# Another order table for attention in thirds and two MLPs: most GpSimd operations go to VectorE and ScalarE

## The chip, the cores and the metric

The kernel runs on one core of a Trainium2 chip. The core has TensorE (PE in the profile, and PEld for its weight loads), VectorE (DVE), ScalarE (ACT), GpSimd (POOL) and SyncE (SP), which here issues every DMA. Each engine has its own queue and takes its instructions strictly in the order in which they stand there. The metric is the device time of one execution in microseconds, the median of several runs.

## The reference, cut to what matters

```python
scores = where(mask[h], (q @ k.T) / sqrt(64), -1e9)      # 4 batches, 8 heads, 576 positions, head size 64
attn   = softmax(scores);  x = attn @ v                  # heads 0-3: 32 last positions; heads 4-7: every 4th of the last 128
x = x.transpose(0, 2, 1, 3).reshape(2304, 512)
x = square(relu(x @ w_in1)) @ w_out1                     # 512 -> 2048 -> 512
h = x @ w_in2
out = (h * sigmoid(h)) @ w_out2                          # 512 -> 2048 -> 512
```

The inputs q, k and v are float32; the weights arrive as float64, which the kernel reads as pairs of 32-bit words.

## The kernel before, in words

**Precision.** Every large matrix product runs as three matmuls of rounded 32-bit operands (fp32r): each factor is split into a high part (a copy that rounds, L238, L240 or L242, by the engine that does it) and a low part (the difference, `sub`, L245), and hi·hi, hi·lo and lo·hi are summed in PSUM. The helper lines L238 to L245 therefore hold most of the elementwise work of the kernel. The tile names tell the uses apart: `w`, `wp` and `st` are weights, `x` and `xs` activations that enter a layer, `g` the hidden activations, and `hl` and `gq` the halves and the hidden blocks in the last part.

**Weights.** A chunk of 128 x 512 float64 weights is turned into float32 in six steps (L275 to L311: scale the upper word, scale the lower word, shift, put the sign in, add the words as integers) and then split. Half of the chunks are also summed in pairs (L363, L382, L410) for products of Strassen's kind, and what is needed later goes out to DRAM (`w1s`, `w1x`, `w2s`, `w2x`, `w2y`) and is read back.

**Stages.** Stage I, from the start to 278 us: most of the attention (48 blocks, each a third of a batch and a pair of heads: scores L515, masked minimum L525, exponential L530, division L534 to L548, transpose L557, product with v L570) woven into the first MLP on its first three column tiles of 192, 320 and 256 (L645 to L695). Stage II, from 278 to 567 us: the other three tiles of the first MLP, 512 columns each, with seven products in place of eight in its first half (L793; the sums of the seven are L807 to L816 on ACT and DVE) and plain products in its second (L847 to L849). Stage III, from 567 us to the end: the second MLP in three tiles of 768 columns, with seven products of 384 columns in both halves (L951 and L1036); L922 and L927 take sums out of PSUM, L987 is the Silu, and L245 on `gq` and `hl` makes the differences and the low parts.

**What sets the order.** Nothing is decided while the kernel runs. The program first makes a list of 3840 operations without order. A text table, `ORDER`, then names them one after another: a letter for the engine (P TensorE, V VectorE, A ScalarE, G GpSimd, D a DMA on SP, F a run of warm-up matmuls), the operation's number, and behind each @ the place of a buffer in SBUF or the PSUM bank. `Planner.order` reads the table, and the operations are issued in that sequence; semaphores between engines follow from the data. Every GpSimd operation gets one wait more: for the last operation on VectorE ahead of it in the table that is marked `lock`, which are those that read or write only SBUF (`o.turn = turn` in `order`, made a dependency at the end of `run`).

Of the kernel before, what the change touches and what calls it, by code (L numbers as in the profile page):

```python
# [1216 lines left out]
G0 V1 D40@145 F15@2 P42@1@65@0 V47 D21@179 P23@0@18@1 D2@160 D59@113 D78@104 D87@196 G88@118 V43 G89 A44 V49 A50  # L1217
A48 V45 V24 A46 V51 V52 A79@154 G81 P61@1@33@3 V64 A65 V68 V28 A69 V53 V62 P4@2@149@2 V7 V26 V66 V5 A63 V9 A29
A8 V90 D350@172 D95@97 F5@3 P351@0@190@0 F14@2 G97 G96@159 G98 D146@22 G147@141 G149 V91 V92 V354 V356 P54@2
F3@1 A67 A6 A27 V70 V71 V352 V72 A25 V30 V31 A10 A80 V11 V12 D129@145 G130@91 V82 G83 G148 G84@0 V33 A355 A353  # L1220
A55 F1@1 V99 A14 V13 P15@3 V100 V16 G101@82 A32 A357 A17 V358 V359 V132 A131 V133 G134 A360 P34@0 A36 A35
D366@137 P367@3@50@2 V372 A373 V368 A369 G85 G135@86 G102 D418@36 P419@2@194@3 V422 V420 D494@114 F2@1
P495@1@128@1 F3@0 V370 A421 A423 P73@0 D163@109 A371 A164@98 D22@41 D121@179 G136 G122@144 G123 V150 V498 V496
V500 V424 V374 V151 V375 V166 V167 V165 F7@3 P361@2 F3@3 A362 A74 D3@52 P37@2 P18@3 V19@4 V20 A501 A376 A499
V168 V38 V39 A152@74 V153 A425 A497 D41@198 P56@1 A57@20 D60@133 P75@3 A76 D112@29 A114 G113@155 V426 V77 V58
D104@151 A105@65 G107 A106 P1118@2 P1124@0 A1119@107 A1120 V124 V427 V428 D138@102 G139@157 G141 G140 V502 V503
A1125@92 A505 V115 V116 V117 G118@44 G119 A1126 A1121@130 G1122 V125 V108 G109 P377@2 P363@1 A364@7 V365 V142
A378 P429@0 A169@30 A430 A1127@15 G170 G126 D382@146 P383@3@12@2 V384 D436@59 P437@2@79@3 V440 A441 V442 V438
A443 A504 V388 A389 A439 V386 V1431@90 D512@167 P513@1@68@0 V516 V390 P1130@0 A1131@165 V514 V518 A519 A1132
V444 V445 V446 P431@2 A432 V434@38 V435 P379@1 V380 V381 V433 G93@34 G94 A517 D400@53 P401@3@150@1 V402 A515  # L1230
V110@48 P447@0 V143 V111 A387 P506@1 A508 A448 A391 P1136@2 A507 A1137@191 A1138 G1139@66 D180@23 D454@109
# [12 lines left out]
A241@203 V552 V490 V491 P1148@2 A1149@196 V493 A195@52 A553 A557 G243 G226 A1150 G1151@181 V1180 G1181@169 V590
V591 A592 D214@121 V215@179 V1444@184 V233 V1440 V235 D206@23 D265@66 A267 G236 G1152 G208 G1445 P1160@3 P1172@1
V216 P593@0 A594 V244 V558 V559 P1184@2 A1185@197 A1161@14 D581 V245 P1153 V266@194 V196 V1170 P1171 A1173@80
A1186 V217 A1174 G268 G1175@145 V560 P561@1 A562 V1446@199 V1162 V218 G207@177 V209 V210 G211 G1447 V1176
A1163@181 V227 V1182 G1448 G237@125 P595@3 D248@172 A249@78 A225 G228 A212@149 D598@117 P599@2@191@3 D634@157
D1438 V219 G220@153 G1466@122 V251 V1164 V596@142 D650@129 D616@70 D1441 V1449 D1450 D188 V606 V602 V604 P563@0
V250 V564 V252 G253 G254@26 G255 A603 A605 A1451 G1452 V221 P1196@1 P1208@3 A1197@12 A1209@173 V565 V213 V269  # L1250
G270 V600 A1187@161 A601 D1453 D274@187 D86 P1165 P1177 P1190@0 P1183 V238 A607 V608 V1198 V609 V610 V1188
A229@137 A1199@15 A1191@179 A1192 G1193@183 V1210 V1467@18 G1200 G230 A1211@96 G1194 G1212 P611@1 V612 P1202@2
A1203@181 V1204 P617@0@23@0 V620 V624 A625 V622 A623 P635@3@165@1 V638 A639 V618 V640 V636 A619 A637 A621 P613@2
A614@192 P1220@1 V626 A641 A1221@90 V1222 V642 V643 P1189 P1214@2@3@0 V1454@12 A644 P645@1 A646 A1215@68
A1205@42 A1216 A1217@198 P1201 V276 V275@175 V277 V278 V627 V271@78 G272 P651@1@177@1 V652 V654 A653 V656 P647@2
V648@179 P1213 G628 P629@2 V246@96 G247 G279 P1226@1 A1227@173 A1228 A655 P1195 V630 P631@1 A632@167 D615 D120
D597 D103 D257@161 D137 D702@117 D308@145 D649 P1232@2 A1233@0 A1234 V1455@165 V1456@200 V1218 G1206 G1470@141
G1457 P1207 P1238@1 V1468@68 V1469 V258@195 G1229@64 G1458@184 V260 V1471 V259 V261 G262 A1235@171 V1236 G1459
A1460 A1475 G1476 G263@161 G1461 A1472 G1473 D282@14 V283@24 V1230 V285 V309@2 G311 A1239@72 A657 V658 V310 D633
A1240 A284 V286 G287 V659 V660 P1244@2 A1245@18 P1231 D666@121 D299@190 A1246 A1247@181 P667@1@82@1 V668 A669  # L1260
V672 V674 V300@188 V670 A671 P1250@2 A1251@179 V1252 G1253@42 P661@1 P1219 V312 A662 A673 A675 V676 V677
P703@2@13@2 V708 V706 P663@1 D291@165 D171 D222 D1477 A1223@169 A678 G264 G1463 G313 V302 A709 G1224 V664@129
P1237 D684@157 D1474 V1254 V704 A705 A707 D1462 D316@171 D665 P1262@1 A1263@196 V710 V288@44 G289 V711 V1464
P679@2 A680 V1264 V314@141 V315 P1255 P685@1@70@3 V692 A712 V690 A691 G301 P681@2 A682@147 V688 V303 G280@64
G1248 V1479@68 A693 V686 V713 V304 P1225 P1256@2 A1257@121 V1258 A293 G305@190 A1241@24 G1242 A687 A1259@178
A689 P1268@1 P1249 P714@2 V292@203 V281 P1243 V294 A1269@199 A1270 G1490@42 A716 A715 P717@2 V295 V296 V694
V1491@168 V317@145 V319 D205 D154 D720@129 G306 A1271@117 G1272 V718@182 V695 V696 P1280@1 A1281@0 A1282 P1286@2
# [257 lines left out]
```

## Time and profile before

| | |
|---|---|
| runs | 955.8, 950.17, 955.35 us (median 955.35) |
| profiled execution | 957.83 us, its span 956.0 us, mean granted TensorE clock 0.966 |
| busy PE / DVE / ACT / POOL | 884.0 / 660.0 / 393.7 / 594.4 us |
| DMA | 227.92 MB, 238 GB/s in the mean |

"Busy" is the time in which an engine has an instruction under way. Matmuls overlap one another, so that a PE that is busy all the time may still run below its best rate; the distance from one matmul's start to the next one's tells the rate. An instruction on DVE or ACT starts some 0.07 us before the recorded end of the one in front of it, so that the steady distance of a group is a little less than its duration. A group's mean holds undisturbed instructions and slowed ones alike; the smallest duration of a group is what an undisturbed one takes.

### The profile page before, as it was taken

The page shows a single profiled execution, that of the slowest core. Times are in us where ns is not written, and L with a number is a line of the kernel's source. Part 1 is how long each engine was busy: PE and PEld are TensorE (multiplying, and loading weights), DVE is VectorE, ACT ScalarE, POOL GpSimd, SP SyncE. Part 2 cuts the span into 40 slices and gives each one's busy share as a digit, 9 for nine tenths or more (in the row PEclk, how much of TensorE's full clock was granted, in tenths as well). Part 3 has the DMA queues.
Part 4 walks back from the last instruction along what each step waited for, and adds up shares of the span by engine and source line. Part 5 has one row for each costly group of instructions (what it writes and reads, how often), then busy time and mean ns, then how long its engine had stood idle before and what let it go on. Part 6 is the DMA issues. An engine that isn't in the chain of part 4 may idle for free. (4 is left out here: it accounts for less than half of the span.)

```text
span 956.0 us, 17592 instructions
## 1 busy us (share of the span) xinstructions
PE 884.0 (92%) x6317; PEld 822.5 (86%) x6317; DVE 660.0 (69%) x1288; ACT 393.7 (41%) x1071; POOL 594.4 (62%) x589
## 2 busy tenths in 40 slices
PE   7898797999899999999999978999999989999988
PEld 5698686999888887898898858898989988999978
DVE  6989968857766578776689997658862376324771
ACT  5655344555344233212211222665324654337730
POOL 5777767668755767364637788767870378503662
PEclk9778998999999999999999998999999999999999
DMA  8625567537979988877988966885676264865441
GB/s 316 229 92 189 167 210 242 174 137 246 333 241 342 321 292 290 297 261 252 337 301 301 312 240 239 322 280 206 238 287 226 96 237 160 308 234 185 154 177 67
DMA packets 87064, 227.92 MB, mean 238 GB/s; under 512 B 8640, under 2 KB 20160, under 8 KB 86976
## 3 DMA queue, kind: packets, MB, share of 16 engines
q1 hardware_dynamic: 86976, 226.79, 68.3%
q8 instruction: 50, 0.82, 0.3%
q14 instruction: 38, 0.31, 0.1%
HBM read 176.42 MB, written 50.33 MB: 237 GB/s over the span
## 5 line engine op out<-in xcount | busy, mean ns | idle before, releaser
L245 POOL TENSOR_TENSOR hl<-gq,hl 128x384 fp32r<-128x384 f32 x78 | 89.5, 1163 | 97.9 <-ACT hl L238 72.8
L951 PE MATMUL y<-xs,ws 128*128 128x384 f32 x552 | 107.4, 335 | 1.6 <-DVE gq L922 0.7
L238 ACT CAST hl<-gq 128x384 fp32r<-128x384 f32 x168 | 77.6, 512 | 72.0 <-POOL gq L245 33.5
L245 DVE TENSOR_TENSOR hl<-gq,hl 128x384 fp32r<-128x384 f32 x90 | 81.2, 931 | 27.6 <-ACT hl L238 27.5
L951 PEld LDWEIGHTS y<-xs,ws 128*128 128x128 f32 x552 | 96.4, 188 | 3.3 <-DVE gq L922 1.5
L530 ACT ACTIVATE ap<-ap,ast 128x80 f32<-128x80 f32 (+3 forms) x168 | 59.1, 353 | 66.1 <-DVE ast L525 56.3
L809 DVE TENSOR_TENSOR h<-s,h 128x512 f32<-128x512 f32 x96 | 59.4, 619 | 37.2 <-PE s L793 22.3
L848 PE MATMUL y<-g,w 128*128 128x512 f32 x192 | 77.2, 402 | 6.0 <-DVE g L245 4.6
L1036 PE MATMUL sa<-hl,wp 128*128 128x384 f32 x432 | 79.7, 336 | 2.4 <-ACT hl L238 1.1
L1036 PEld LDWEIGHTS sa<-hl,wp 128*128 128x128 f32 x432 | 75.1, 188 | 3.6 <-ACT hl L238 1.4
L245 POOL TENSOR_TENSOR gq<-gq 128x384 f32<-128x384 f32 x49 | 56.0, 1155 | 34.3 <-DVE hl L245 22.6
L245 POOL TENSOR_TENSOR g<-r,g 128x512 fp32r<-128x512 f32 (+3 forms) x54 | 62.6, 1165 | 23.4 <-ACT g L238 6.0
L793 PE MATMUL s<-x,ws 128*128 128x256 f32 x576 | 76.8, 284 | 0.3 <-DVE x L245 0.3
L847 PE MATMUL y<-g,w 128*128 128x512 f32 x192 | 76.9, 400 | 0.0
L849 PE MATMUL y<-g,w 128*128 128x512 f32 x192 | 76.3, 398 | 0.0
L922 DVE TENSOR_TENSOR gq<-y,gq 128x384 f32<-128x384 f32 x46 | 25.2, 552 | 73.8 <-PE y L951 57.3
L927 ACT COPY gq<-y 128x384 f32<-128x384 f32 x92 | 42.9, 481 | 78.5 <-PE y L951 78.2
L793 PEld LDWEIGHTS s<-x,ws 128*128 128x128 f32 x576 | 73.1, 192 | 1.7 <-DVE x L245 0.5
L645 PE MATMUL s<-x,w 128*128 128x192 f32 (+2 forms) x192 | 59.9, 312 | 4.2 <-DVE xo L240 4.2
L1036 PE MATMUL sa<-hl,sw 128*128 128x384 f32 x288 | 53.6, 339 | 9.3 <-DVE hl L245 6.5
L1036 PEld LDWEIGHTS sa<-hl,sw 128*128 128x128 f32 x288 | 49.7, 188 | 12.4 <-DVE hl L245 8.4
L242 POOL TENSOR_SCALAR g<-r 128x512 fp32r<-128x512 f32 (+3 forms) x41 | 27.3, 666 | 52.1 <-DMA raw<-w 9.2
(165 smaller groups left out, 2431.4 us busy)
## 6 DMA issues: line engine op xcount, KB each, us to landing
raw<-w SPq DMA_DIRECT2D x64, 512.0 KB, 5.8
ws<-w1x SPq DMA_DIRECT2D x48, 512.0 KB, 6.3
ws<-w2x SPq DMA_DIRECT2D x48, 512.0 KB, 6.0
sw<-w2y SPq DMA_DIRECT2D x48, 512.0 KB, 4.8
wa<-w1s SPq DMA_DIRECT2D x24, 512.0 KB, 5.7
wa<-w2s SPq DMA_DIRECT2D x24, 512.0 KB, 5.9
blk<-qkv SPq DMA_DIRECT2D x16, 512.0 KB, 6.4
w1x<-st SPq DMA_DIRECT2D x16, 512.0 KB, 5.0
```

What stands on the lines that cost most here:

```text
L238: self.nc.scalar.copy(out=out, in_=in_)
L245: self.eng[eng].tensor_tensor(out=out, in0=a, in1=b, op=ALU.subtract)
L530: es.append(self.op({"ACT": c_act(nk) + 0.185}, lambda e, i=i, c=c: nc.scalar.activation(out=p.tile[:, c], in_=p.tile[:, c], func=AF.Exp, ...
L645: nc.tensor.matmul(o, wh.tile[:, s], xh, start=(kk == 0), stop=False)
L793: nc.tensor.matmul(bank.tile[:, o:o + 256], wp, xp, start=i == 0, stop=last, skip_group_check=True)
L809: add = lambda o, a, b: nc.vector.tensor_tensor(out=o, in0=a, in1=b, op=ALU.add)
L847: nc.tensor.matmul(o, wh.tile[:, s], gh.tile, start=c == 0, stop=False)
L848: nc.tensor.matmul(o, wh.tile[:, s], gl.tile, start=False, stop=False)
L849: nc.tensor.matmul(o, wl.tile[:, s], gh.tile, start=False, stop=(c == NF - 1))
L927: return self.op({"ACT": c_actp(half)}, lambda e: nc.scalar.copy(out=out(), in_=bank.tile[:, :half]), deps, key, allocs, uses + [bank])
L951: nc.tensor.matmul(o, w[part == 2].tile[:, kk * P:kk * P + P], x[b][part == 1].tile[:, kk * half:kk * half + half], start=new and not kk a ...
L1036: nc.tensor.matmul(o, u.tile[:, c * P:c * P + P], v.tile, start=new and not q and not part, stop=q == nf - 1 and part == 2, skip_group_che ...
```

## The change

Only the table is another. The list of operations, what each computes, and all other code are the same. The new table names the same 3840 operations and the same nine runs of warm-up matmuls (53 in all).

| | operations before | after |
|---|---|---|
| TensorE, DMA | 746, 540 | 746, 540 |
| VectorE | 1120 | 1457 |
| ScalarE | 874 | 1020 |
| GpSimd | 560 | 77 |
| stage I: VectorE, ScalarE, GpSimd | 455, 331, 197 | 565, 427, 19 |
| stage II | 388, 182, 181 | 463, 222, 28 |
| stage III | 277, 361, 182 | 429, 371, 30 |

In all, 695 operations have another engine than before; 32 of them go to GpSimd. Of what leaves GpSimd, differences and sums (two operands) go to VectorE: `hl` 78 to 18 on GpSimd, `gq` 49 to 3, `w`, `wp` and `st` low parts 61 to 13, the integer adds of L311 30 to 2, the sums of L363, L382 and L410 59 to 9, the low parts of `g` 54 to 6. Rounding copies and scalings (one operand) go for the most part to ScalarE: `g` 41 to 4 on GpSimd, `st` and `w` copies 51 to 3, the two scalings of the weights 45 to 3. Of the shifts of L295/L297, 20 go from GpSimd to VectorE. In stage I the operations of VectorE grow by 110: by 60 of two operands and 512 columns, by 41 that are of one operand and 512 columns or of two operands and 256, by 22 low parts of `g`, less 13 that are for the most part copies out of PSUM given to ScalarE. No operation of TensorE is issued more than 25 places earlier or later among the 746 than before; most keep their place or move by one or two. The places of the buffers in SBUF are others throughout.

```diff
@@ ORDER @@
-G0 V1 D40@145 F15@2 P42@1@65@0 V47 D21@179 P23@0@18@1 D2@160 D59@113 D78@104 D87@196 G88@118 V43 G89 A44 V49 A50
+G0 D21@181 P23@2@8@1 V1 V24 A25 V28 V26 A29 A27 D40@137 P42@0@11@0 V43 V45 A46 A44 V47 A48 D95@166 V97 V49 A50
...
```

The first place is the conversion of the first weights, for which the first matmuls of the first MLP (L645) wait. A stretch near the start of GpSimd's queue before (`cv` a converted chunk, `raw` a chunk as loaded, `w_309` a chunk's high and low part):

```order
L285 TENSOR_SCALAR raw<-raw 128x512
L242 TENSOR_SCALAR w_309<-cv 128x512
L242 TENSOR_SCALAR w_328<-cv 128x512
L311 TENSOR_TENSOR cv<-cv,raw 128x512
L245 TENSOR_TENSOR w_309<-cv,w_309 128x512
L242 TENSOR_SCALAR w_368<-cv 128x512
L245 TENSOR_TENSOR w_328<-cv,w_328 128x512
L245 TENSOR_TENSOR w_368<-cv,w_368 128x512
```

VectorE's queue after, at the same work (`x` is the input of the first MLP, `ax` a PSUM bank of the attention):

```order
L295 TENSOR_SCALAR cv<-cv 128x512
L534 TENSOR_SCALAR ast<-ast 128x3
L245 TENSOR_TENSOR x<-ax,x 128x192
L311 ISA cv<-raw,cv 128x1024
L536 RECIPROCAL ast<-ast 128x3
L285 TENSOR_SCALAR raw<-raw 128x512
L240 CAST w_547<-cv 128x512
L245 TENSOR_TENSOR x<-ax,x 128x4x48
```

The scalings, integer adds, copies and differences of the weights now stand between the attention's steps in one queue, where before GpSimd had a good part of them in a queue of its own.

The second place is the second half of the last tile of the second MLP, where the matmuls of L1036 wait for `hl`. The end of GpSimd's queue before:

```order
L245 TENSOR_TENSOR gq<-gq 128x384 x2
L245 TENSOR_TENSOR hl<-gq,hl 128x384 x2
L245 TENSOR_TENSOR gq<-gq 128x384 x2
L245 TENSOR_TENSOR hl<-gq,hl 128x384 x5
L245 TENSOR_TENSOR gq<-gq 128x384
L245 TENSOR_TENSOR hl<-gq,hl 128x384 x6
L245 TENSOR_TENSOR gq<-gq 128x384
L245 TENSOR_TENSOR hl<-gq,hl 128x384 x3
```

VectorE's queue after, near its end (`yq` is a block of the output, summed out of PSUM):

```order
L245 TENSOR_TENSOR gq<-gq 128x384 x5
L245 TENSOR_TENSOR hl<-gq,hl 128x384 x2
L245 TENSOR_TENSOR gq<-gq 128x384
L245 TENSOR_TENSOR hl<-gq,hl 128x384 x5
L245 TENSOR_TENSOR gq<-gq 128x384
L245 TENSOR_TENSOR hl<-gq,hl 128x384 x5
L922 TENSOR_TENSOR yq<-sa,yq 128x384
L245 TENSOR_TENSOR gq<-gq 128x384
L245 TENSOR_TENSOR hl<-gq,hl 128x384 x2
```

What GpSimd and VectorE did side by side here is now nearly all in VectorE's queue, in one row with the sums out of PSUM; GpSimd keeps 7 `hl` and one `gq` of this tile.

## Rows read from the trace of the kernel before

**Rows 1.** The page, part 1: busy us, share of the span, instructions.
```profile
PE 884.0 (92%) x6317; PEld 822.5 (86%) x6317; DVE 660.0 (69%) x1288; ACT 393.7 (41%) x1071; POOL 594.4 (62%) x589
```

**Rows 2.** Busy time by stretch, I, II, III: length, engines, clock, DMA share, GB/s.
```profile
0.00:278.00 278.00, 243.93 (x2294) 223.67 (x2295) 219.70 (x584) 136.14 (x477) 195.01 (x219) 0.91 0.62 214
278.00:567.00 289.00, 279.21 (x2009) 246.42 (x2008) 221.70 (x422) 78.21 (x230) 178.30 (x180) 0.99 0.86 297
567.00:956.00 389.00, 360.89 (x2017) 352.38 (x2015) 218.57 (x284) 179.31 (x364) 221.05 (x191) 0.99 0.61 213
```

**Rows 3.** The chain of waits: start, us, work.
```profile
721.81 6.24 PE y L951 x36
```

**Rows 4.** PE in order of time: start, us, instructions.
```profile
318.14 0.40 PE L847 MATMUL y<-g,w 128*128 128x512 f32 x1
...
319.98 0.39 PE L849 MATMUL y<-g,w 128*128 128x512 f32 x1
...
410.83 3.17 PE L793 MATMUL s<-x,ws 128*128 128x256 f32 x24
413.83 0.88 PE L793 MATMUL s<-x,wc 128*128 128x256 f32 x6
```

**Rows 5.** Line L245: duration ns smallest/median/largest, first and last start, forms.
```profile
L245 DVE TENSOR_TENSOR hl<-gq,hl x90: 540/768/2176, 607.6 to 944.7; 128x384 fp32r<-128x384 f32 x90
L245 POOL TENSOR_TENSOR hl<-gq,hl x78: 996/1062/1663, 620.4 to 938.3; 128x384 fp32r<-128x384 f32 x78
L245 DVE TENSOR_TENSOR st<-st x22: 660/692/1782, 92.4 to 633.5; 128x512 fp32r<-128x512 f32 x22
```

**Rows 6.** Line L922, the same view: sums that read PSUM.
```profile
L922 DVE TENSOR_TENSOR gq<-y,gq x46: 542/556/558, 594.1 to 891.7; 128x384 f32<-128x384 f32 x46
```

**Rows 7.** DVE and POOL in order of time, second half of a tile.
```profile
788.10 6.50 DVE L245 TENSOR_TENSOR hl<-gq,hl 128x384 fp32r<-128x384 f32 x5
...
791.57 3.91 POOL L245 TENSOR_TENSOR hl<-gq,hl 128x384 fp32r<-128x384 f32 x3
...
895.13 1.03 DVE L245 TENSOR_TENSOR hl<-gq,hl 128x384 fp32r<-128x384 f32 x2 [2.44 <-ACT hl L238]
```

**Rows 8.** DVE groups of stage I: busy us, mean ns | idle before, releaser.
```profile
L307 DVE SCALAR_TENSOR_TENSOR cv<-cv,raw 128x512 int32<-128x512 int32 x16 | 19.6, 1224 | 0.6 <-POOL raw L297 0.6
L304 DVE SCALAR_TENSOR_TENSOR cv<-raw,cv 128x512 int32<-128x512 int32 x20 | 17.7, 885 | 0.3
L542 DVE TENSOR_TENSOR ap<-ap,ast 128x192 f32<-128x192 f32 (+2 forms) x21 | 16.5, 788 | 0.4
L534 DVE TENSOR_SCALAR ast<-ast 128x3 f32<-128x3 f32 (+1 forms) x34 | 15.5, 455 | 4.2 <-ACT ap L530 4.1
...
L245 DVE TENSOR_TENSOR w<-cv,w 128x512 fp32r<-128x512 f32 x14 | 14.0, 1002 | 1.5 <-POOL w L242 0.7 <-ACT w L238 0.7
L295 DVE TENSOR_SCALAR cv<-cv 128x512 int32<-128x512 int32 x20 | 12.6, 631 | 2.2 <-POOL cv L277 2.0
```

**Rows 9.** Lines L295 and L534: duration ns smallest/median/largest.
```profile
L295 DVE TENSOR_SCALAR cv<-cv x34: 412/427/1501, 10.8 to 603.2; 128x512 int32<-128x512 int32 x34
L534 DVE TENSOR_SCALAR ast<-ast x48: 134/170/1303, 7.3 to 417.3; 128x4 f32<-128x4 f32 x24, 128x3 f32<-128x3 f32 x24
```

**Rows 10.** Busy time by stretch, around the end of stage II.
```profile
504.00:576.00 72.00, 61.59 (x343) 53.85 (x342) 68.76 (x78) 15.32 (x28) 57.68 (x50) 0.96 0.80 275
```

**Rows 11.** The page, part 5: ACT's rounding copy in stage III.
```profile
L238 ACT CAST hl<-gq 128x384 fp32r<-128x384 f32 x168 | 77.6, 512 | 72.0 <-POOL gq L245 33.5 <-DVE gq L245 14.0 <-POOL hl L245 8.1
```

**Rows 12.** Whom DVE and PE waited for: us in total, times, longest.
```profile
DVE gq L922 <- PE y L951: 57.3, 20, 6.1
...
DVE hl L245 <- ACT hl L238: 27.5, 13, 4.0
DVE ap L525 <- PE ax L515: 25.6, 16, 4.6
...
PE sa L1036 <- DVE hl L245: 7.1, 7, 1.6
```

More of the change, by code (lines that the diff above doesn't have):

```diff
@@ L1222 @@
[L1222 to L1231, printed above, removed]
@@ new lines @@
+P449@2 V452 V109 A409 V520 V521 V523 A1139@12 A407 V522 V410 V411 V412 V453 A457 A186@113 P509@3 A510 V511
+P395@1 F3@0 A396 A450 A463 V1134 V1140 G187 P1142@0 A1143@170 V451 A110@48 A1144 A127@100 A459 P1154@1 A1155@92
+A1145@23 A461 A174 A1156 A173@149 A1157@163 G1158 D530@125 V111 P531@3@54@1 V536 V128 V538 A539 D197@154
+V198@146 D566@159 P567@0@151@2 V572 V570 V464 V160 V200 V532 P397@2 P1129 P1135 V175 V568 V534 V176 A144@60
+D474@199 P475@1@96@0 A199 V465 V145 V1146 P524@0 V525 A161@92 V162 A526 A537 A535 A573 V177 A569 V466 P413@3
@@ new lines @@
+P1196@3 A1197@80 P1208@1 P1153 V606 V221 V209 V241@191 A607 V243 P1165 P1171 V1176 P1177 A1187@177 A1209@200
+V1182 V210 V238 A592 P593@2 A1210 A267 A225 V211 A212@149 V251 A266@163 A1198 V244 V1444@196 V245 V213 P1183
+V1445 A605 V608 V1188 V1446@16 V609 V1447 V250 A246@96 V252 D616@70 D634@157 P635@3@180@2 V640 P617@1@193@0
+D274@64 D1441 V636 V638 V268 V622 V253 V228 A1448 A1199@174 A594 P595@0 A596@161 P1190@2 V247 V620 V610
+A1191@131 A1192 V254@26 P1202@0 A1203@186 A1204 A1205@42 P1189 V1449 A1211@171 V255 A1193@165 V618 V1194 V1200
@@ new lines @@
+P1297 D342@198 D1498 D1535@86 D324 D1501 D1554@74 A1329@176 A343@72 A1330 A1537 A1325@0 A1536@183 V1512 V1308
+P1334@1 A1335@185 P1309 V345 V339@113 D790@30 D1510 D755 V786 D1513 V767 V768 P769@2 V1531 A1331@121 A1336
+V1514@166 V1332 V1326 P1333 V346 V770 V340 V1515@23 V1516@56 P787@1 A788@14 V1517 A1337@122 P791@2@70@0 V1538
+V792 P771@1 V772@187 A793 V796 V1338 D773 P1327 V794 A795 A344 V1518@117 V1519 V1532@129 V1533 V347 V348@145
+V1539 V1540 A1523 V1524 A797 V798 D1534 D341 D806@198 D1525 D1563@179 P1310@1 A1520 A1311@5 A1312 P1340@2
@@ new lines @@
+A1341@194 A1342 A1313@68 A1343@202 P1352@1 A1353@185 A1354 V799 V800 P1346@2 A1347@86 A1348 A1349@171 V1314
+P1358@1 V1544@129 A1359@165 V349 V1556 V1541@1 V1542 A1360 P801@2 A802 P1339 P803@1 A1555@173 A804@32 V1344
+V1546@125 V1521 V1557 P807@2@88@3 V808 A809 V1350 V812 V1545 A1548 V814 A813 V810 A1355@118 V1356 P1364@1
+A1365@10 V1366 V1547 A1367@7 V1368 A815 D824@185 D805 D1958@22 P1345 P1370@2 P1376@1 A811 V816 V817 V1549 V818
+G1551 V1552 A1564@72 V1565 A1361@183 V1566 A1371@42 A1372 A1373@12 A1377@79 A1378 P819@2 A820 P1315 P1357
@@ new lines @@
+D2585 D2635@44 P2763 V1949 D2641@183 P2766 D1739 D1928 A2764 V1950@125 V2830 A2802@191 V1951 V2751 V2767 V1939
+A1952 V1953 D2642@153 P2768 D2644@195 P2770 P2772 V2773 V2817 V2824 A2765 A1955 A2805@70 V2854 V2803 V1956
+A2769@47 A2812@44 V2813 V2862 V2850 A2771@14 P2775@3 P2777 A2758 A2825@118 A2778 A2774 V2806 V2836 D2639@106
+D1905 P2779 A2780 A2781 A2851@67 A2855@80 A2808@54 A2960@41 D2645@148 P2782 D2643@77 D1954 P2784 V2785 P2804
+A2837@148 A2884@115 P2787 A2788 A2948@61 V2856 V2776 A2789 V2809 V2826 V2840 A2841@196 V2783 V2832 V2858
@@ L1461 @@
+V3762 P3768@1@3 P3771 P3774 V3822 A3823@151 V3824 A3803@16 V3804 V3764 V3728 D3729 P3777 P3780 P3783 P3786
+A3811@35 V3812 P3789 P3797 P3801 P3805 P3809 P3813 V3792 V3726 D3727 D3763 D3765 V3790 D3791 D3793 V3816 P3817
+P3821 P3825 P3828 P3829 A3826@181 D3827 P3830 P3831 P3832 P3833 P3834 P3835 A3836 D3837
 """
```

448 lines of the change are left out of this document (215 added, 233 removed).

## The prediction

> **What bounds the kernel now.** The page's first part says TensorE: it is busy for 92% of the span [rows 1]. That share hides how well it runs, so the next view is busy time by stretch for the three stages [rows 2], set against what the matmuls need at their best rate. In stage III, 36 matmuls of 384 columns follow one another in 6.24 us, 0.1733 us each [rows 3]; the stage has 2016 of them (L951 and L1036, 3 tiles x 8 pairs of chunks x 42 each; 2017 matmuls in all [rows 2]), which is 349.4 us, and it takes 389. In stage II, eight distances between matmuls of 512 columns are 319.98 - 318.14 = 1.84 us, 0.23 each, and 24 of 256 columns take 413.83 - 410.83 = 3.00, 0.125 each [rows 4]: 576 (3 tiles x 16 chunks x 12) and 1008 (3 x 8 x 42) of them are 132 + 126 = 258 us, and with the 425 small matmuls of attention left in the stage (2009 - 1584 [rows 2]), at an estimated 0.03 us, about 270; it takes 289. In stage I the 1152 large matmuls (3 tiles x 16 chunks x 24, 256 columns in the mean) are 144 us, and the rest is small ones; the granted clock is 0.91 there, against 0.99 later. With 0.91 as a mean of full and half speed, 0.18 of 278 us, 50 us, went at 1.2 GHz, and at 2.4 GHz would have taken 25 less: stage I needs between 144 and 244 - 25 = 219 us of TensorE, and takes 278. The excess over TensorE is then about 59 or more, 19 and 40 us.
>
> Why TensorE waits there, the rows of VectorE tell. In stage I VectorE is busy for 219.7 of 278 us [rows 2]. But its instructions do not take what they need. The difference of 384 columns on two SBUF operands takes 540 ns at the least, 768 at the median, 2176 at the most [rows 5]; a sum of the same width that reads PSUM takes 542, 556, 558 [rows 6], never slowed. In order of time the reason shows: five `hl` on VectorE take 6.50 us, 1.29 each, while GpSimd's three beside them take 3.91, 1.30 each; two `hl` with GpSimd idle take 1.03, which is 0.47 from start to start [rows 7]. Side by side the two engines step in turn, one operation each per 1.3 us. The same two in one row on VectorE take 0.94.
>
> **The change, part by part.** *Relief of what VectorE has.* In stage I the slowed groups, mean less undisturbed duration [rows 8, 9]: L307 16 x (1.224 - 0.68) = 8.7; L304 20 x 0.205 = 4.1; `w` 14 x 0.32 = 4.5 (0.68 by the 660 to 692 of the same width [rows 5]); L295 20 x 0.21 = 4.2; L534 34 x (0.455 - 0.16) = 10.0 (0.16 between its smallest and its median); L542 21 x (0.788 - 0.43) = 7.5, with 0.43 estimated between 540 at 384 columns and its own 192 to 320. These six are 39 us of 95.9 busy. The other 124 us hold between nothing and the same share, 51; I take 26, half, since about half of them read PSUM and are not slowed [rows 6]. So 65 us fall away, within 39 and 90: 219.7 becomes 155.
>
> *What VectorE gets.* In stage I, 110 operations net: 60 of two operands at 0.61 us start to start (0.68 less the 0.07 by which the next one starts early), 41 at 0.34 (0.41 [rows 9] less the same), the rest about +3 us: 37 + 14 + 3 = 54. Its need becomes 209 us, within 184 and 235. With 19 GpSimd operations left there, each can still hold VectorE up once: between 0 and 15 us, 3 taken, since the start of the run, with the constants, holds some of them.
>
> *How full VectorE can run.* When it is what all wait for, it is busy for 68.76 of 72 us, 95.5% [rows 10]. 209 / 0.955 + 3 = **222 us for stage I**, just above TensorE's upper bound of 219, against 278.
>
> *Stage II.* VectorE gets 75 operations, at most 46 us at 0.61: 221.7 + 46 = 268 even with no relief at all, under TensorE's 270. TensorE sets this stage; of the 19 us of excess I keep 5: **275 us**. The transfers move the same bytes; GB/s rise from 297 to 297 x 289 / 275 = 312 and the DMA share from 0.86 to 0.90, close to its end but not over.
>
> *Stage III.* 152 operations more on VectorE, nearly all of 384 columns at 0.47, are 71 us: 218.6 + 71 = 290 without relief, against 349 of TensorE. The rows that are on the path are the `hl` before L1036 [rows 12] and the differences before them: in the stretches like [rows 7], 1.3 us per pair become 0.94. What stays of the 40 us is the wind-down after the last matmul (3.5), the starts of the three tiles and of their second halves, where TensorE waits for a chain ACT to VectorE whatever its rate: 15 in all. 349.4 + 3.5 + 15 = **368 us**.
>
> *ScalarE* gets 146 operations at 0.5 us (a rounding copy takes 512 ns [rows 11]), 73 us: 394 becomes 467, half of the span. In stage I it is 136 + 96 x 0.45 = 179 of 222, under VectorE; what hides it is VectorE's queue, and if that were empty TensorE's 219 would still cover it. *TensorE's and SyncE's queues* carry the same operations in nearly the same order; shifted matmuls and moved buffers are set at nothing, hidden by the work queued on TensorE, between -5 and +5 us a stage if a buffer comes free earlier or later.
>
> Sum: 222 + 275 + 368 = 865, and 1.8 around the span is 867, against the profiled 957.8. That execution lies 2.5 above the median of the runs, 955.35, so the time is about 865.
>
> One rule speaks against the change. In the rows, an instruction of 0.55 us is followed by the next after 0.47 us [rows 7], so that VectorE loses nothing between two of its own. The Trainium skill, page "VectorE: DVE Perf Modes", section "The DRAIN you can't avoid", says that after each Vector instruction the next does not start until the pipeline is empty, and adds that one that is not held starts earlier. By its first half more instructions on VectorE would cost more than their work; the two rows above agree with the second half.
>
> **Rivals.** *Full durations.* If each of VectorE's instructions held the queue for its whole duration in a dense row, 0.075 us come on top of each: (584 + 110) x 0.075 = 52 in stage I, whose need is 261, and 273 + 3 = 276 us; II and III stay under TensorE. That is 918. [rows 7] speak against it. Chance 4%. The page's rule named above is this case.
>
> *The relief reaches only stage I.* If TensorE's waits in II and III come from chains between engines and from transfers, not from slow operations, three quarters of the excess stay: 222 + 284 + 379, about 884. For it: in stage III each of the waits [rows 12] is short, and DMA is at 0.86 in II. Against it: those chains are made of the same slowed operations. Chance 18%.
>
> *Off the path.* The slowed operations were hidden, and the table in effect only changes who is idle: 950. Against it is that VectorE is the busiest engine after TensorE just where TensorE is slowest. Chance 4%.
>
> *Slower: work stuck behind waits in one queue.* VectorE waits in order: 57 us for L951, 26 for L515, 28 for ACT's `hl` [rows 12], and idles 956 - 660 = 296 us in all. Before, GpSimd went on with weights and halves meanwhile. Now these stand behind the waiting instruction, and TensorE behind them. VectorE's work after is 660 less about 30% relief by stage I's share (65 of 220, 195 in all) plus 54 + 40 + 71 = 630; the change loses if its idle time grows from 296 to above 325. That needs some 30 us more of waits: 15 of the 106 differences moved in stage III late by the mean wait of 2.9 us (57.3 / 20) are 43, and then the time is 630 + 296 + 43 = 969, with what lies around it about 970. It decides against the change only where all old waits stay as well; since most of these are VectorE idle beside a busy TensorE, shorter spans shrink them. Chance 8%.
>
> **How the numbers follow.** The forecast has 66%. The predicted time is 865. Low: VectorE without a pause in I (209), 272 and 362: 842. High: stage I at its upper need, 235 / 0.955 + 3 = 249, with 280 and 380: 909, which takes in the rival of 884. Outside lie most of 950, 970 and 918. What a measurement can tell from no change is about 1%. Faster by over 1%: 66 + 18 + 4 = 88%; within 1%: 4%; slower: 8%.
>
> **What would show it.** Right: `hl` and `gq` on VectorE near 0.55 us in the mean, from 0.93; VectorE's busy time between 600 and 690 in spite of 337 more operations; stage I ending at 215 to 235; the granted clock there above 0.95. Wrong: VectorE's means still above 0.8 with GpSimd nearly idle (then it was not GpSimd that slowed them), TensorE waiting over 2 us at a time for `hl` or `g` on VectorE (the one queue), or a DMA share of 0.95 in stage II (transfers).

## The result, and the profile after

The changed kernel takes 877.08 us in the median (875.97 to 878.07, 4 runs) against 953.79 (950.17 to 955.8, 4 runs): a ratio of 0.9199, 95% interval 0.9166 to 0.9233. The forecast was 865 with a range of 842 to 909. The profiled execution is 876.68 us, its span 874.9. One execution of all that follow, of 1416.8 us at a granted clock of 0.62 (the run with one input), is left out of its median.

The page's first part answers [rows 1]:

```profile
PE 850.3 (97%) x6317; PEld 801.7 (92%) x6317; DVE 661.4 (76%) x1625; ACT 469.7 (54%) x1230; POOL 90.4 (10%) x87
```

VectorE runs 337 instructions more than before in the same busy time, 661.4 us for 660.0. GpSimd's busy time fell from 594.4 to 90.4 us, and ScalarE has 76 us more. The busy time by stretch answers [rows 2], with the boundaries where stages II and III begin now (length, then busy us and instructions of PE, PEld, DVE, ACT and POOL, then clock, DMA share, GB/s):

```profile
0.00:234.00 234.00, 219.61 (x2253) 204.24 (x2254) 204.41 (x676) 172.31 (x567) 18.79 (x29) 0.98 0.72 250
234.00:515.00 281.00, 277.47 (x2045) 247.47 (x2045) 230.91 (x521) 110.42 (x290) 29.55 (x28) 1.00 0.89 310
515.00:875.00 360.00, 353.23 (x2023) 349.97 (x2021) 226.04 (x429) 187.00 (x376) 42.09 (x30) 1.00 0.66 229
```

Stage I lost 44 us, II 8, III 29. The columns tell how: length less TensorE's busy time is its idle time, and that fell from 34.1 to 14.4 us in I, from 9.8 to 3.5 in II, from 28.1 to 6.8 in III, 47 us in all. The other 34 us are TensorE's busy time itself, 884.0 to 850.3 with the same 6317 matmuls: the granted clock rose from 0.91 to 0.98 in stage I and from 0.99 to 1.00 in the two others. By these clocks an estimate, (1 - clock) x length, gives 32 us lost before and 5 after, so that the clock makes some 27 of the 34; the other 7 are not traced. So TensorE had lost time in two ways, idle and with matmuls at the lower of the clock's two levels (1.2 GHz in place of 2.4).

Line L245 answers [rows 5] (duration ns smallest/median/largest):

```profile
L245 DVE TENSOR_TENSOR hl<-gq,hl x150: 544/551/1376, 549.8 to 864.5; 128x384 fp32r<-128x384 f32 x150
L245 DVE TENSOR_TENSOR gq<-gq x93: 543/551/1374, 550.7 to 854.7; 128x384 f32<-128x384 f32 x93
L245 DVE TENSOR_TENSOR st<-st x45: 661/685/1600, 84.3 to 577.6; 128x512 fp32r<-128x512 f32 x45
L245 POOL TENSOR_TENSOR hl<-gq,hl x18: 1009/1028/4186, 546.8 to 841.0; 128x384 fp32r<-128x384 f32 x18
```

The smallest duration of `hl` on VectorE is what it was (540 before); its median came down from 768 to 551, to the smallest. The mean is 582 ns where it was 931, that of `gq` 560. That is the effect in one row: the work did not get cheaper, it is no longer held up. In order of time four of them in one row keep the distance that [rows 7] showed only while GpSimd was idle, (1.95 - 0.55) / 3 = 0.47 us:

```profile
612.21 1.95 DVE L245 TENSOR_TENSOR hl<-gq,hl 128x384 fp32r<-128x384 f32 x4
```

### The profile page after: what moved, and what is told of

Its sections match the earlier page's. It is cut to its first block, busy times and chain, and to the rows that moved or that the text cites. A ratio compares the mean times of both kernels' runs of the same rounds, so it can differ in the third digit from the quotient of the medians.

```text
span 874.9 us, 17358 instructions
## 1 busy us (share of the span) xinstructions
PE 850.3 (97%) x6317; PEld 801.7 (92%) x6317; DVE 661.4 (76%) x1625; ACT 469.7 (54%) x1230; POOL 90.4 (10%) x87
## 4 chain that ended last, share of the span: by engine, by line
PE 47%; DVE 9%; issue 4%; DMA 4%; ACT 1%; POOLq 1%; POOL 0%; SPq 0%; DVEq 0%; ACTq 0%
PE y L951 16%; PE sa L1036 10%; PE s L793 6%; PE sa L951 3%; PE y L1036 3%; PE y L848 3%; PE y L847 3%; PE y L849 3%; DVE hl L245 2%; DMA sw<-w2y 1%; DVE h L809 1%; DMA raw<-w 1%; DVE gq L245 1%; DMA out<-yq 1%; DVE cv L311 1%
## 5 line engine op out<-in xcount | busy, mean ns | idle before, releaser
L245 DVE TENSOR_TENSOR hl<-gq,hl 128x384 fp32r<-128x384 f32 x150 | 81.9, 582 | 9.2 <-ACT hl L238 9.0
L1036 PE MATMUL sa<-hl,wp 128*128 128x384 f32 x432 | 78.9, 335 | 0.4 <-DVE hl L245 0.4
L922 DVE TENSOR_TENSOR gq<-y,gq 128x384 f32<-128x384 f32 x46 | 25.3, 554 | 68.6 <-PE y L951 55.3
L530 ACT ACTIVATE ap<-ap,ast 128x96 f32<-128x96 f32 (+3 forms) x168 | 59.4, 355 | 31.3 <-DVE ast L525 31.0
L848 PE MATMUL y<-g,w 128*128 128x512 f32 x192 | 75.5, 393 | 0.4 <-DVE g L245 0.3
L1036 PEld LDWEIGHTS sa<-hl,wp 128*128 128x128 f32 x432 | 75.1, 188 | 0.9 <-DVE hl L245 0.7
L238 ACT CAST g<-r 128x512 fp32r<-128x512 f32 (+3 forms) x92 | 45.8, 506 | 55.8 <-DVE r L829 26.9
L847 PE MATMUL y<-g,w 128*128 128x512 f32 x192 | 75.6, 394 | 0.0
L849 PE MATMUL y<-g,w 128*128 128x512 f32 x192 | 74.9, 390 | 0.0
L793 PE MATMUL s<-x,ws 128*128 128x256 f32 x576 | 74.8, 283 | 0.1
L645 PE MATMUL s<-x,w 128*128 128x192 f32 (+2 forms) x192 | 58.1, 303 | 0.5 <-DVE x L245 0.3
L245 DVE TENSOR_TENSOR g<-r,g 128x512 fp32r<-128x512 f32 (+3 forms) x90 | 49.7, 561 | 9.6 <-ACT g L238 9.0
L646 PE MATMUL s<-x,w 128*128 128x192 f32 (+2 forms) x192 | 56.5, 294 | 0.0
L647 PE MATMUL s<-x,w 128*128 128x192 f32 (+2 forms) x192 | 56.4, 294 | 0.0
L245 DVE TENSOR_TENSOR gq<-gq 128x384 f32<-128x384 f32 x93 | 50.0, 560 | 5.4 <-ACT gq L987 3.7
L1036 PE MATMUL y<-hl,sw 128*128 128x384 f32 x288 | 51.7, 335 | 0.9 <-POOL hl L245 0.9
```

The source lines that it names most:

```text
L238: self.nc.scalar.copy(out=out, in_=in_)
L245: self.eng[eng].tensor_tensor(out=out, in0=a, in1=b, op=ALU.subtract)
L530: es.append(self.op({"ACT": c_act(nk) + 0.185}, lambda e, i=i, c=c: nc.scalar.activation(out=p.tile[:, c], in_=p.tile[:, c], func=AF.Exp, ...
L645: nc.tensor.matmul(o, wh.tile[:, s], xh, start=(kk == 0), stop=False)
L646: nc.tensor.matmul(o, wh.tile[:, s], xl, start=False, stop=False)
L793: nc.tensor.matmul(bank.tile[:, o:o + 256], wp, xp, start=i == 0, stop=last, skip_group_check=True)
```

## The experiments

The kernels differ from the changed one in letters of the table (`V1158` is operation 1158 on VectorE, `G1158` the same on GpSimd) or in the lines shown. The medians of the kernel before in these sessions were 952.2 to 953.3 us, and the ratios are to them.

### Engines or order

Each half of the change alone. First the new order and places with the old engines (695 letters, three of them here):

```diff
-V97 V49 A50 V96@142 V98
+G97 V49 A50 G96@142 G98
```

> The changed kernel's table, its order and places kept, with all 695 operations that changed engine put back on the engine of the kernel before. If the engines made the gain (some 500 us of GpSimd's two-input work that held VectorE up), nearly all of it is lost: 930 to 970 us, the 150 late products hl on VectorE's side near 0.9 us again, GpSimd busy near 590 us. If the order and the places made it: 875 to 900 us.

Measured: 1030.3 us, ratio 1.0846 (1.081 to 1.0883). It is outside what both theories gave, and slower than the kernel before. The signs named for the first theory are there: GpSimd is busy for 573.7 us, and `hl` on VectorE has a mean of 884 ns, although the median is now near the smallest:

```profile
L245 DVE TENSOR_TENSOR hl<-gq,hl x90: 541/568/1634, 654.2 to 1009.9; 128x384 fp32r<-128x384 f32 x90
```

All three stages are longer than before, 305, 313 and 410 us for 278, 289 and 389. VectorE waits for GpSimd for 114 us in all (49 before) and for ScalarE for 106 (79): as these waits suggest, the new order asks the old engines for results before they are there. Then the old order and places with the new engines (the edit is to the kernel before):

```diff
-G97 G96@159 G98 D146@22 G147@141
+V97 V96@159 V98 D146@22 V147@141
```

> The table of the kernel before, its order and places kept, with the engines of the changed kernel for those 695 operations. If the engines made the gain: 880 to 910 us, the rest up to 877 being what the order is worth once it fits the engines. If order and places made it: 940 to 960 us.

Measured: 998.53 us, ratio 1.0498 (1.0472 to 1.0524). The theory that the engines make the gain falls in this form: by themselves, at the old places, they lose 5%. Yet VectorE is relieved in this kernel as in the changed one. The rows of the page's part 5 (busy us, mean ns | idle before, releaser) of this kernel, then of the changed one:

```profile
L245 DVE TENSOR_TENSOR hl<-gq,hl 128x384 fp32r<-128x384 f32 x150 | 79.8, 563 | 55.2 <-ACT hl L238 55.1
```

```profile
L245 DVE TENSOR_TENSOR hl<-gq,hl 128x384 fp32r<-128x384 f32 x150 | 81.9, 582 | 9.2 <-ACT hl L238 9.0
```

The mean is 563 ns, undisturbed. What differs is the idle time ahead: 55 us of VectorE standing before an `hl` whose rounding copy ScalarE has not made, against 9. In the old order these differences were spread over two queues, each with time for the copy in front; put in one queue at the same places they wait for it one after another, and what stands behind them waits as well. The same holds for other rows: VectorE's waits for ScalarE come to 167 us in this kernel and 52 in the changed one, and that is nearly all by which its idle time differs (331 us and 214). The stretches of its three stages:

```profile
0.00:283.00 283.00, 232.33 (x2226) 212.33 (x2228) 200.69 (x662) 168.82 (x556) 18.26 (x28) 0.91 0.58 200
283.00:593.00 310.00, 287.89 (x2083) 255.36 (x2078) 238.06 (x537) 109.59 (x296) 29.05 (x29) 0.99 0.81 286
593.00:996.00 403.00, 364.04 (x2016) 355.68 (x2014) 226.56 (x428) 188.01 (x378) 44.32 (x30) 0.97 0.59 205
```

VectorE's busy time in stage III is the changed kernel's, 226.6 and 226.0, and the stage takes 403 us in place of 360; I and II are 49 and 29 us longer too. Given the new engines, the order and the places together are worth 998.5 - 877.1 = 121 us; given the new order, the engines are worth 153. Neither is worth anything alone. How much of the 121 is the order and how much the places of the buffers was not separated.

### One stage back

The changed kernel with stage III's 195 changed operations on their old engines:

> The changed kernel with only the 195 changed operations of stage III (the last stretch, the attention's second half and the output) back on their old engines. If each stage's gain comes from its own operations: stages I and II end where they end in the changed kernel (234 and 515 us, within 3), stage III takes 380 to 392 us in place of 360, so 897 to 909 us in all, and hl on VectorE has a mean near 0.9 us there. If the stages share one gain through the order (III is fed early by I and II): under 885 us.

```diff
-V2800 V2830 G2794
+G2800 G2830 V2794
```

Measured: 926.3 us, ratio 0.9738 (0.9708 to 0.9768). The stages:

```profile
0.00:239.00 239.00, 224.47 (x2251) 209.81 (x2252) 203.87 (x676) 172.41 (x566) 19.08 (x29) 0.95 0.70 244
239.00:520.00 281.00, 277.45 (x2045) 247.39 (x2044) 230.65 (x522) 110.14 (x291) 29.49 (x28) 1.00 0.88 309
520.00:928.00 408.00, 371.87 (x2025) 358.85 (x2023) 209.11 (x288) 181.24 (x367) 203.58 (x180) 0.97 0.58 203
```

Stage II is the same to the microsecond, and III takes 48 us more, beyond the 20 to 32 expected: with this order its old engines cost more than the stage gained over before (29), as in the run with all engines back. `hl` on VectorE has a mean of 892 ns again. So the gain of III is its own and not a gift of the earlier stages. Stage I has the same operations as in the changed kernel and took 5 us more; its TensorE was busy 4.9 us longer, at a clock of 0.95 for 0.98. That much a single trace of stage I can differ by without any change in it.

### Does GpSimd hold VectorE up, or is it only slow?

Two theories explain the kernel before. By the one, GpSimd's instructions hold up VectorE's (the prediction's). By the other, they are only slow, 1.03 us for 0.47, for those who wait for their results. First GpSimd without any work but the constants (76 letters):

```diff
-G1158 ... G2052
+V1158 ... V2052
```

> The changed kernel with its last 76 operations on GpSimd (all but the constants) given to VectorE (69) and ScalarE (7). If what is left on GpSimd still slows VectorE (90 us of spans, in which a VectorE subtraction costs about 1.3 us in place of 0.5): 870 to 876 us. If TensorE bounds all three stages by now, as its busy share of 97% has it: 874 to 880 us, no difference. If VectorE is short again (69 more operations, some 40 us): over 885 us.

Measured: 886.28 us, ratio 0.933 (0.9304 to 0.9355), 9 us slower than the changed kernel. VectorE's rows:

```profile
L245 DVE TENSOR_TENSOR hl<-gq,hl x168: 545/550/560, 557.5 to 876.9; 128x384 fp32r<-128x384 f32 x168
L245 DVE TENSOR_TENSOR gq<-gq x96: 545/549/559, 562.0 to 867.1; 128x384 f32<-128x384 f32 x96
```

Of 264 instructions not one takes over 560 ns: without GpSimd's work no slow one is left. Its stages II and III take 281 and 362 us, for 281 and 360 in the changed kernel; nearly all of the loss is in stage I (245 us for 234, in an execution 3.5 us above the median), which the last experiments take up.

On this kernel a load was put on GpSimd that nobody waits for:

```diff
+                    for _ in range(3):
+                        self.nc.gpsimd.tensor_tensor(out=idle, in0=self.ident, in1=self.ident, op=ALU.subtract)
```

behind every locked `hl` and `gq` on VectorE (they are all 264, not the 243 of the expectations), behind every second of them, and with two other instructions in its place.

> The kernel without GpSimd work (886 us, its hl and gq subtractions on VectorE 545 to 560 ns, the slowest too), with work on GpSimd that nobody waits for: behind each of the 243 locked late subtractions on VectorE in stage III, three subtractions of two 128x128 inputs on GpSimd (about 1.2 us together, by 1.03 us for 128x384). If GpSimd's reading of two inputs holds VectorE up whoever waits: hl and gq on VectorE rise to a mean of 0.8 us or more, stage III takes 20 to 80 us longer than its 361 us. If GpSimd was only a slow producer for those behind it: hl and gq stay at 0.55 us and the time within 1% of 886.

Measured: 1025.25 us, ratio 1.0769 (1.0731 to 1.0807). This time misleads: GpSimd had not finished its own load when the kernel's work was done. The last matmul ends at 918.4 us, the last of the load at 1018.6; in the kernel without the load the last matmul ends at 883.8. From the first matmul of stage III to the last it takes 395.2 us (from 523.2) against 357.6 (from 526.2). The load nobody waits for costs 38 us, and VectorE's rows say by what:

```profile
L245 DVE TENSOR_TENSOR hl<-gq,hl x168: 543/750/775, 554.6 to 911.5; 128x384 fp32r<-128x384 f32 x168
L245 DVE TENSOR_TENSOR gq<-gq x96: 548/749/765, 559.6 to 901.8; 128x384 f32<-128x384 f32 x96
L1180 POOL TENSOR_TENSOR idle<-ident x792: 398/400/1988, 555.3 to 1018.2; 128x128 f32<-128x128 f32 x198
```

A piece in order of time:

```profile
859.48 1.42 DVE L245 TENSOR_TENSOR hl<-gq,hl 128x384 fp32r<-128x384 f32 x2
859.89 6.65 POOL L1180 TENSOR_TENSOR idle<-ident 128x128 f32<-128x128 f32 x10
860.82 1.42 DVE L245 TENSOR_TENSOR gq<-gq 128x384 f32<-128x384 f32 x2
862.17 0.75 DVE L245 TENSOR_TENSOR hl<-gq,hl 128x384 fp32r<-128x384 f32 x1
862.84 0.75 DVE L245 TENSOR_TENSOR gq<-gq 128x384 f32<-128x384 f32 x1
```

Five distances from start to start on VectorE, from 859.48 to 862.84, are 0.67 us each, ten instructions on GpSimd in 6.65 are 0.67 each: again the two step in turn, one instruction each, as in [rows 7]. The second theory falls as the whole explanation: GpSimd holds VectorE up whoever waits for it. What its slowness as a producer cost besides, in the kernel before, was not separated.

> The same with three subtractions on GpSimd behind every second of the 243, half the dose. If GpSimd's two-input reads hold VectorE up: about half as many of the subtractions on VectorE are slowed, and stage III grows by 5 to 35 us, less than with the full dose. Otherwise within 1% of 886 us.

Measured: 926.01 us, ratio 0.9721 (0.9684 to 0.9758); from the first matmul of stage III to the last 394.9 us. Half the load costs the same 37 us, against the expectation, and the median of `hl` is 750 ns again. While VectorE has differences in a row it starts one each 0.67 us and GpSimd can do no more than one instruction for each; both loads bring more than that (three and 1.5). By that, which is argued and was not varied further, GpSimd is busy in either case where it hurts, and the rest of its work falls where VectorE does other things or nothing.

> The same as the full dose, but GpSimd's three instructions behind each of the 243 are memsets of 128x128, which read nothing. If it is the reading of two inputs that holds VectorE up: hl and gq stay near 0.55 us and the time within 1% of 886 us. If any GpSimd instruction that touches the memory does: hl and gq rise and stage III grows by 10 us or more. If what costs is the signalling from VectorE to GpSimd at 243 places: the same loss here as with the two-input load.

```diff
-self.nc.gpsimd.tensor_tensor(out=idle, in0=self.ident, in1=self.ident, op=ALU.subtract)
+self.nc.gpsimd.memset(idle, 0.0)
```

Measured: 888.83 us, ratio 0.9337 (0.9302 to 0.9372), as without a load. Stage III from its first to its last matmul takes 356.5 us. The signals from VectorE to GpSimd, the same in number, cost nothing:

```profile
L245 DVE TENSOR_TENSOR hl<-gq,hl x168: 547/551/561, 557.5 to 875.9; 128x384 fp32r<-128x384 f32 x168
L1180 POOL MEMSET idle<- x792: 204/205/449, 558.1 to 886.3; 128x128 f32 x198
```

> The kernel without GpSimd work, with the idle load of the full dose (three GpSimd instructions behind each late subtraction on VectorE, 792 in all), but each multiplies one 128x128 input by a constant in place of subtracting two. If only GpSimd's reading of two inputs holds VectorE up: hl and gq on VectorE stay at 0.55 us and the time is 884 to 893 us, as with the memsets. If any reading does: hl and gq rise toward the 0.75 us of the two-input load and the work of stage III ends 15 us or more later.

```diff
-self.nc.gpsimd.tensor_tensor(out=idle, in0=self.ident, in1=self.ident, op=ALU.subtract)
+self.nc.gpsimd.tensor_scalar(out=idle, in0=self.ident, scalar1=1.0, scalar2=1.0, op0=ALU.mult, op1=ALU.mult)
```

Measured: 947.62 us, ratio 0.9939 (0.9911 to 0.9967), again with GpSimd's own rest behind the work: the last matmul ends at 895.9 us, and stage III takes 369.6 from its first, 12 us more than without a load. That one input costs nothing is wrong; that it costs 15 us or more was a little too much:

```profile
L245 DVE TENSOR_TENSOR hl<-gq,hl x168: 542/639/676, 557.7 to 889.0; 128x384 fp32r<-128x384 f32 x168
L1180 POOL TENSOR_SCALAR idle<-ident x792: 299/300/1880, 558.4 to 944.1; 128x128 f32<-128x128 f32 x198
```

```profile
868.95 7.03 POOL L1180 TENSOR_SCALAR idle<-ident 128x128 f32<-128x128 f32 x13
869.20 2.88 DVE L245 TENSOR_TENSOR hl<-gq,hl 128x384 fp32r<-128x384 f32 x5
```

Five on VectorE keep (2.88 - 0.64) / 4 = 0.56 us, thirteen on GpSimd 0.54. So three kinds of GpSimd instruction give a step of 1.30 [rows 7], 0.67 and 0.56 us for the pair. Undisturbed, GpSimd's recorded durations are 1.03, 0.40 and 0.30, and VectorE's distance from start to start is 0.47: in each the pair takes the sum of both less about 0.2. The memset of 0.2 fits that as well as it fits that it reads nothing; these runs do not tell the two apart.

### Where the rest of stage I is

Stage I ended at 234 us where 222 was predicted. Two of VectorE's conversion steps were made narrow, so that most of the first weights stay unconverted (one of the edits):

```diff
-out=vi(), in0=vi(), in1=pair(I32)[:, :, 0], op=ALU.add)
+out=vi()[:, :None if m else 8], in0=vi()[:, :None if m else 8], in1=pair(I32)[:, :, 0][:, :None if m else 8], op=ALU.add)
```

> The changed kernel with two of VectorE's in-place steps in the conversion of the first weight matrix (L304 or L307, and L311) done on 8 columns in place of all 512: part of the computation is left out, some 49 us of VectorE's work in stage I goes, of it about 18 us between 12 and 60 us, 11 between 60 and 100, 19 after 100. If VectorE bounds stage I throughout: it ends 30 us or more earlier than 234 us. If VectorE bounds only its first 100 us and TensorE the rest: it ends 8 to 25 us earlier, all of it gained by 100 us. If TensorE and the first transfers bound it: 5 us at most.

Measured: 875.42 us, ratio 0.9191 (0.9155 to 0.9227); stage I ends at 235.0 us, though VectorE's busy time in it fell from 204.4 to 172.0:

```profile
0.00:235.00 235.00, 223.88 (x2253) 208.67 (x2254) 171.99 (x676) 170.47 (x566) 16.50 (x29) 0.96 0.72 248
```

VectorE does not bound it. In the first 36 us it did help: the first large matmul (L645) starts at 27.8 us in place of 32.9. Then the five microseconds go. Two stretches of 24 us of this kernel, and of the changed one:

```profile
48.00:72.00 24.00, 23.90 (x235) 22.12 (x235) 13.03 (x65) 16.33 (x62) 1.87 (x2) 0.72 0.66 228
72.00:96.00 24.00, 23.87 (x245) 22.37 (x244) 20.74 (x79) 21.82 (x70) 1.66 (x2) 1.00 0.59 178
```

```profile
48.00:72.00 24.00, 22.38 (x289) 20.09 (x288) 22.86 (x90) 20.99 (x79) 2.68 (x3) 1.00 0.69 233
72.00:96.00 24.00, 23.70 (x234) 22.39 (x233) 23.34 (x73) 21.65 (x65) 2.15 (x2) 1.00 0.59 192
```

With VectorE at half load TensorE is busy throughout the first of them and yet does 235 matmuls, of mixed sizes, for 289, because the clock is 0.72. Over stage I it is idle for 3.3 us less than in the changed kernel and busy for 4.3 us more. That is this execution: the four have clocks of 0.988, 0.994, 0.994 and 0.988 and take 877.15, 873.7, 872.74 and 878.49 us, the changed kernel at 0.994 takes 876.68 and 875.97. So where the clock held, some 3 us of the earlier start were kept. Why it falls in some executions is not shown.

So the clock was tried: 44 more filler matmuls (the trace has 6361 for 6317; the expectation says 43) in the idle stretches of the first 25 us.

```diff
-G0 D21@181 P23@2@8@1 V1 ... P42@0@11@0 ... F1@1 ... P34@0 ... P15@1
+G0 D21@181 V1 F13@0 P23@2@8@1 ... P42@0@11@0 F14@3 ... F4@1 ... P34@0 F4@1 ... P15@1 F10@2
```

> The changed kernel with 43 more of its filler matmuls (each about 0.21 us of TensorE and read by nobody) in TensorE's five idle stretches before 25 us: 13 before the first scores, 14 in the 3.4 us before the third, 3 and 4 in short ones, 10 in the 2.4 us ahead of the transposes at 24.5 us. If the idle start is what takes the clock down between 24 and 48 us (0.66 and 0.91 there): the clock there is above 0.85, stage I ends 3 to 10 us earlier than 234 us, the time is 867 to 874 us. If VectorE's work sets the pace there, or the clock falls anyway: 875 to 879 us.

Measured: 876.65 us, ratio 0.9188 (0.9164 to 0.9211), the same as the changed kernel; stage I ends at 233.8 us. The clock between 24 and 48 us is 0.79 with and without them:

```profile
24.00:48.00 24.00, 23.34 (x265) 19.86 (x264) 22.88 (x82) 20.97 (x77) 3.49 (x3) 0.79 0.56 207
```

```profile
24.00:48.00 24.00, 22.49 (x245) 18.95 (x246) 22.18 (x79) 20.19 (x76) 3.68 (x3) 0.79 0.58 210
```

TensorE was busy for 17.5 of the first 24 us in place of 13.6. Filling these idle stretches did not keep the clock up. The second theory of that expectation names two causes, and which of them it is stays open.

Last, what GpSimd is still good for. It keeps its ten operations of the first 60 us and loses the 66 behind:

> The changed kernel with GpSimd keeping only its ten operations in the first 60 us; the other 66 go to VectorE and ScalarE as in the kernel without GpSimd work (886 us, stage I to 245 us, II 281 us, III 361 us). If the 9 us lost there were lost at the start, where GpSimd helps while VectorE is short: 873 to 879 us, stage I to 234 us. If they were lost to the later 66 operations: 883 us or more. If those 66 hold VectorE up where TensorE waits for it: under 873 us.

```diff
-G1158
+V1158
```

This is the first of the 66 letters. Measured: 884.81 us, ratio 0.9279 (0.9257 to 0.93). The expectation of the first theory is missed: stage I ends at 240.3 us although its first 60 us have the old letters. The place shows in order of time, here VectorE at 60 us, and in the changed kernel GpSimd:

```profile
59.68 0.36 DVE L245 TENSOR_TENSOR g<-r,g 128x192 fp32r<-128x192 f32 x1 [3.94 <-ACT g L238]
59.96 0.68 DVE L245 TENSOR_TENSOR w<-cv,w 128x512 fp32r<-128x512 f32 x1
```

```profile
60.66 0.73 POOL L245 TENSOR_TENSOR g<-r,g 128x192 fp32r<-128x192 f32 x1 [2.84 <-ACT g L238]
```

It is operation 1158, the low part of `g`, one of the 32 that the change took to GpSimd. In either queue it waits 3 to 4 us for ScalarE's copy. On GpSimd nobody stands behind it. On VectorE the low part of a weight does, and TensorE waits for that one:

```profile
PE y L695 <- DVE w L245: 2.0, 1, 2.0
```

After it the clock falls; the stretch from 60 to 72 us here, then in the changed kernel:

```profile
60.00:72.00 12.00, 11.30 (x95) 10.59 (x97) 10.41 (x47) 6.04 (x23) 0.00 (x0) 0.72 0.72 235
```

```profile
60.00:72.00 12.00, 12.00 (x152) 11.27 (x152) 11.73 (x42) 10.67 (x41) 0.73 (x1) 1.00 0.92 308
```

VectorE waits 5.8 us for `g` between 44 and 100 us in this kernel and not at all in the changed one. How much of the 6 us of stage I is these waits and how much the clock stays open, since the clock also fell there in the run with stage III's engines back, without these waits, and stage I ended at 239 us. The loss itself is beyond such scatter: the fastest of the five executions takes 883.33 us, the slowest of the changed kernel 878.07.

> The changed kernel with GpSimd keeping only its 20 operations of one input (the five of them before 60 us too); the 56 of two inputs go to VectorE. If GpSimd's help at the start is worth its hold-up of VectorE in either form: stage I ends between 234 and 245 us and the time is 877 to 886 us. If the subtractions on GpSimd cost VectorE as much as they save: 874 to 878 us, as in the changed kernel.

Measured, with GpSimd keeping only its 20 operations of one input: 886.64 us, ratio 0.9304 (0.9276 to 0.9331), stage I to 241.1 us. Just above the first theory's range; the same wait for `g` stands in it (5.2 us), so it says little of the forms of instruction. No version that does the whole computation was faster than the changed kernel beyond the noise.

## Why the prediction was right, point by point

**What holds VectorE up** was GpSimd, as argued from [rows 5 to 7]: shown three ways, by the durations after, by their return with a load nobody waits for, and by their absence with no load. The Trainium skill, page "SBUF — State Buffer", section "SBUF: two separate sides", says that the two engines share a pair of ports, and that a GpSimd instruction and a VectorE instruction with two inputs from SBUF (where GpSimd reads SBUF too) lock each other out for a whole instruction. The steps in turn agree with it, and so does the hold-up by an instruction with one input. The step of the pair, about 0.2 us less than VectorE's distance and GpSimd's recorded duration together, is shorter than "whole" would have it, as far as GpSimd's recorded durations can be trusted.

**VectorE's need in stage I**, 209 us (184 to 235), was 204.4. Its two parts can be worked out from the groups of both traces in stage I. With the changed kernel's mean for each group of the kernel before, the relief is 56 us for the 65 forecast (31 for the 39 of the six groups, 25 for the 26 of the rest), and by the same means the additions are 50 us for 54: both a little smaller, and partly cancelling. Three of the six groups, as the view of [rows 8] has them now (mean ns 885, 455 and 788 before):

```profile
L304 DVE SCALAR_TENSOR_TENSOR cv<-raw,cv 128x512 int32<-128x512 int32 x32 | 23.4, 730 | 0.3
L534 DVE TENSOR_SCALAR ast<-ast 128x3 f32<-128x3 f32 (+1 forms) x33 | 5.4, 162 | 2.9 <-ACT ap L530 2.8
L542 DVE TENSOR_TENSOR ap<-ap,ast 128x192 f32<-128x192 f32 (+2 forms) x21 | 9.2, 439 | 0.3
```

**The step from it to the stage's end failed:** "209 / 0.955 + 3 = 222". VectorE was busy for 204.4 of 234 us, 87%, and taking 32 us of its work away left the end where it was (235.0). The bound is TensorE, whose need the prediction put between 144 and 219 us: it was the upper end, 219.6 us busy. On top come 14.4 idle, of them 11.7 in the first 36 us, where TensorE waits for the first transfers (L515 for `w` of q, k and v, 6.7 us) and the first softmax (L557 for L542, 2.4 us):

```profile
0.00:12.00 12.00, 4.54 (x59) 3.73 (x59) 4.35 (x34) 5.72 (x25) 2.70 (x13) 1.00 0.79 262
12.00:24.00 12.00, 9.05 (x75) 6.72 (x75) 11.69 (x40) 9.07 (x33) 4.16 (x4) 1.00 1.04 405
24.00:36.00 12.00, 10.69 (x109) 8.69 (x110) 11.16 (x36) 9.89 (x37) 1.03 (x1) 0.66 0.69 258
```

A start like this belongs to no engine's need and should have been a term of its own: 219.6 + 14.4 is the 234.

**The signs** named ahead came out: `hl` and `gq` at 0.58 and 0.56 us in the mean, VectorE busy for 661 us (600 to 690), stage I to 234 (215 to 235), its clock 0.98 (above 0.95).

**Stage II**, 275 predicted, took 281: the floor of "about 270" set the small matmuls at 0.03 us, for which no row was given, and TensorE's busy 277.5 less 258 for the large ones gives 19.5 / 461 = 0.042. The DMA share of 0.89 and 310 GB/s were forecast at 0.90 and 312. **Stage III**, 368 predicted, took 360: of 15 us for the starts of tiles and halves 7 were there (360 - 349.4 - 3.5). The misses of +12, +6 and -8, which partly cancel, are 10 of the 12 us between 865 and 877; the rest is the 2.5 us by which the profiled run of before lay above its median, which the one of after does not (876.68 against 877.08).

**Rivals.** Full durations: the distance of 0.47 us in a row excludes it. Relief in stage I only: stage III's 29 us exclude it. Off the path, 950: the time excludes it. **Work stuck behind waits in one queue**, priced at 970 with a chance of 8%, is real: with the old order it is what the change does, at 998.5 us, and VectorE's idle time is then 331 us, above the 325 that this rival named as its sign (214 in the changed kernel). The prediction did not see how much hangs on the order. It set what is shifted at nothing, "between -5 and +5 us a stage", and priced the engines alone; the sum came out because the table had been rearranged so that VectorE rarely stands before an `hl` (9 us for 55). That it would was not argued from any row; in this the prediction was lucky.

## What to carry to other kernels

Set a group's mean and median beside its smallest duration: where either is far above it, someone may be holding the engine up, and a load that nobody waits for shows who. The median alone can miss it (568 ns beside a mean of 884, with the old engines in the new order). When work changes engine, give it a new place as well: the old places suit the old engines. Each half of this change alone loses, 46 and 78 us, where both together gain 77. An instruction that waits is better put in a queue where nothing urgent stands behind it, even a slow one.

## What had not been expected of the hardware

A GpSimd instruction with one input from SBUF holds VectorE's differences up as one with two does, by its own duration less about 0.2 us (0.09 us for one of 0.30, 0.20 for one of 0.40, 0.83 for one of 1.03), and half the load on GpSimd cost as much as all of it (37 and 38 us). An earlier start of TensorE did not shorten stage I in the trace: with its first large matmul 5 us earlier, the clock stood at 0.72 between 48 and 72 us, and stage I ended 1 us later than without. In executions whose clock held at 0.994, some 3 us of it were kept.
